# Attention and a mixer on one core: 128 stationary columns for the scores, a spread-out first pair, and block sums issued elsewhere

## The chip, the cores and the metric

The kernel runs on one core of one Trainium2 chip. The metric is the device time of one execution in microseconds (us). Each kernel was run several times; "fast" runs alone are compared, and all runs here were of that state or single.

Words used below: a *pair* is two heads of attention, and also the two score matmuls of them that run side by side; a *score group* is four score matmuls, that is two such pairs one after the other. A *row tile* is the part of the array's 128 rows that a matmul uses: 64 rows for a score matmul, 128 for most others. The *excess* between two matmuls is the distance of their starts less the steady distance of such matmuls. The *first-layer stretch* and the *output stretch* of a batch are its parts before and after the first matmul of the second layer. The *gain* is the multiplication of a transposed q by the norms' weights on DVE.

## The reference, cut to what matters

```python
def _attn_ref(q, k, v, g_q, g_k):            # q, k, v: 8 batches, 12 heads, 448 tokens, 64 per head
    q_n, k_n = rmsnorm(q, g_q), rmsnorm(k, g_k)
    scores = 1/sqrt(64) * q_n @ k_n.T
    attn = softmax(scores)
    return attn @ v

def _moe_ref(x, U, V, w_ch1, w_ch2):         # x: 8 x 448 x 768, the attention's output
    u = x + (x.T @ U @ V).T                  # mixing over tokens, rank 32
    return u + relu(u @ w_ch1) @ w_ch2       # 768 -> 3072 -> 768
```

## The kernel before

Everything runs in bf16 on the tensor engine (PE). While PE does the two layers of batch b, the attention of batch b+1 is woven in: a list of small items (scores of a pair of heads, exponentials on ScalarE (ACT), values, norms on VectorE (DVE)) with weights is spread over a share `FA` of the layers' work. A batch has six pairs of heads; p counts pairs over all batches.

```python
P, SP, D = 128, 112, 64
FA, FM, NPE, FA0 = (0.74, 0.77), 0.09, 14, 0.66

def scores(p, kcs):                          # two heads of 64 rows each, side by side in the array
    qT, kT = qkTs[p][:, 0], qkTs[p][:, 1]
    for kc in kcs:
        sc = ps_s.tile([SP, 2, 512], FP32, tag="s")
        for hh in range(2):
            pp = slice(hh * D, (hh + 1) * D)
            nc.tensor.matmul(sc[:, hh, 0:S], kT[pp, kc * SP:(kc + 1) * SP], qT[pp, :], start=True, stop=True)
        scs[p, kc] = sc

def gains(p):                                # DVE, after the transposing DMA of pair p has landed
    if p >= NPE:
        nc.vector.tensor_scalar(qkTs[p][:, 0], qkTs[p][:, 0], gg, None, OP.mult)

def attention(b, extra={}):                  # ... cut to the items that matter here
    for p in range(b * 6, b * 6 + 6):
        add(2 if p == 6 else 1, scores, p, (0, 1))
        add(0, expo, p, 0)
        add(.5, expo, p, 1)
        if p + 1 < NP and (p + 1 >= NPE or not odd):
            add(.5, transposes, p + 1)       # for p + 1 >= NPE a transposing DMA
        # ...
        if p % 6:
            add(2, values, p - 1, 0)         # matmuls into o, then DVE: reciprocal, x, xs
        # ...
        add(1, scores, p, (2, 3))
        add(0, expo, p, 2)
        add(.5, expo, p, 3)
        # ...
        if p + 1 < NP:
            add(0, gains, p + 1)
        # ...
        if p % 6:
            add(1.5, values, p - 1, 1)
```

The second layer of most rows is done by a scheme of seven block products in place of eight (`pair`), which needs sums of blocks of the activations hT on DVE:

```python
def act_sums(i, c0, c1):
    A11, A21, A22 = (hTe[:, c0:c1, k, t * P:(t + 1) * P] for k, t in ((0, i), (0, i + 1), (1, i + 1)))
    nc.vector.tensor_tensor(S1[:, c0:c1], A21, A22, OP.add)
    nc.vector.tensor_tensor(A21, A21, A11, OP.subtract)

def mlp(b):
    for hc in range(0 if b else 4, KH):      # first layer, 24 pieces of 128 columns
        # ... six matmuls into ph; even hc: relu on ACT, odd hc: relu on DVE
        if b and hc in (7, 15, 21, 23):
            act_sums(0, *{7: (0, 4), 15: (4, 8), 21: (8, 11), 23: (11, 12)}[hc])
        yield n
    # ... second layer: odd batches (N=512) two pairs, even ones (N=384) a single block row and a pair
    #     yield from pair(b, 0, lambda: act_sums(2, 0, NC))
```

## Time and profile before

| | before |
|---|---|
| median time, 6 runs beside the changed kernel | 587.84 us (586.63 to 591.5) |
| profiled execution, span | 584.4 us, granted clock 1.0 in all slices |
| busy: PE, DVE, ACT | 565.6, 395.0, 279.1 us |
| score groups on PE (outside the head) | 84 |

The page's first lines and its chain of waits, of the kernel before; the busy line gives us, share of the span and count:

```profile
PE 565.6 (97%) x4613; PEld 313.4 (54%) x4613; DVE 395.0 (68%) x811; ACT 279.1 (48%) x413; POOL 78.3 (13%) x122
...
PE 82%; DVE 11%; ACT 4%; issue 1%; DMA 1%; POOL 1%; DVEq 0%; POOLq 0%; ACTq 0%
```

PE is the bound. But "97% busy" is not "97% streaming", since a matmul's duration overlaps the next one's. The useful number is the distance from one matmul's start to the next. In steady state a 128x384 matmul follows another after 162 ns, although each is given 326 ns. Where the distance is larger, PE lost time. For the scores that happens three times per group. The timeline of the kernel before around one score group (start, us, engine, line, operation, idle of that engine before it):

```profile
332.43 0.67 PE L299 MATMUL o<-va,E 112*128 112x65 bf16 x16
333.03 0.18 PEld L273 LDWEIGHTS <-qkT 64*112 64x112 bf16 x4
333.03 0.58 PE L273 MATMUL sc<-qkT 64*112 64x448 bf16 x4
...
333.55 1.74 PEld L477 LDWEIGHTS <-w1b 128*128 128x128 bf16 x12 [0.34 <-issue]
333.55 2.12 PE L477 MATMUL ph<-u,w1b 128*128 128x384 bf16 x12
```

The weight load of the next matmul normally starts together with the matmul before it. Here the load after the group sat idle for 0.34 us for no reason that the profile shows ("issue"), and so did the first load of most groups. The groups of instructions of the kernel before (busy us, mean ns, then idle time of the engine before them):

```profile
L477 PEld LDWEIGHTS <-w1b 128*128 128x128 bf16 x1128 | 103.0, 98 | 106.6 <-issue 20.1
...
L273 PE MATMUL sc<-qkT 64*112 64x448 bf16 x384 | 60.0, 373 | 5.7 <-DVE rec L302 2.1
...
L273 PEld LDWEIGHTS <-qkT 64*112 64x112 bf16 x384 | 19.3, 124 | 37.3 <-issue 32.7
```

The score loads take 124 ns for 112 columns, the others 98 ns for 128: fewer columns, longer. And here are the waits of PE that have a named cause (total us, times, longest):

```profile
PE sc L273 <- DVE rec L302: 2.1, 3, 0.9
PE sc L273 <- DVE qkT L265: 1.7, 3, 0.6
PE o L299 <- DVE xs L306: 1.6, 3, 0.5
PE sc L273 <- ACT E L278: 1.2, 4, 0.4
```

The first two come once each in batches 2, 4 and 6 (second and first pair of the next batch's attention), the third once each in batches 1, 3 and 5 (value outputs behind the 0.94 + 1.55 us of block sums). One wait of DVE itself matters later, at the gain, for the transposing DMA:

```profile
DVE qkT L265 <- DMA qkT<-qkn: 2.3, 3, 0.9
```

### The profile page before, as it was taken

How to read it: one execution, taken by the hardware profiler on the slowest of the kernel's cores; microseconds unless marked ns; L12 is line 12 of the kernel's file. 1: busy time of each engine (PE TensorE's matmuls, PEld its weight loads, DVE VectorE, ACT ScalarE, POOL GpSimd, SP SyncE). 2: the span in 40 equal slices, each digit the busy share in tenths (PEclk: the TensorE clock that was granted, in tenths of full speed). 3: DMA queues.
4: the chain of work that ended last, by engine and by line, in shares of the span. 5: the costliest groups of instructions: out<-in, count | busy, mean ns of one | idle time of the engine just before them, and what ended most of it. 6: DMA issues, size and time to landing. Idle time of an engine off the chain costs nothing.

```text
span 584.4 us, 11372 instructions
## 1 busy us (share of the span) xinstructions
PE 565.6 (97%) x4613; PEld 313.4 (54%) x4613; DVE 395.0 (68%) x811; ACT 279.1 (48%) x413; POOL 78.3 (13%) x122
## 2 busy tenths in 40 slices
PE   7899999999999999999999999999999999999997
PEld 2465556544555556544555555644455555654464
DVE  5868987399775788656776588746677477453452
ACT  4957661276622774176631766256651475302200
POOL 4652411000020000000020001000011000000010
PEclk9999999999999999999999999999999999999999
DMA  9999999352554446525545355646425441040021
GB/s 218 244 239 235 223 152 203 82 112 47 106 156 103 110 102 134 139 61 115 118 119 101 75 125 127 148 98 127 109 54 147 94 96 33 28 109 0 1 55 54
DMA packets 103648, 67.22 MB, mean 115 GB/s; under 512 B 54716, under 2 KB 102060, under 8 KB 103596
## 3 DMA queue, kind: packets, MB, share of 16 engines
q1 hardware_dynamic: 93988, 56.77, 41.9%
q0 software_dynamic: 9376, 9.44, 9.9%
q8 instruction: 36, 0.59, 0.4%
q10 hardware_dynamic: 232, 0.30, 0.2%
q14 instruction: 16, 0.13, 0.1%
HBM read 52.19 MB, written 11.01 MB: 108 GB/s over the span
## 4 chain that ended last, share of the span: by engine, by line
PE 82%; DVE 11%; ACT 4%; issue 1%; DMA 1%; POOL 1%; DVEq 0%; POOLq 0%; ACTq 0%
PE ph L477 33%; PE pb L404 8%; PE po L404 8%; PE o L299 8%; PE pa L404 7%; PE sc L273 7%; PE pe L404 6%; ACT E L278 3%; DVE qkn L244 2%; PE pu L337 2%; DVE rstd L231 1%; PE warm L741 1%; DVE hT L400 1%; DVE S L399 1%; DVE x L303 1%
## 5 line engine op out<-in xcount | busy, mean ns | idle before, releaser
L477 PE MATMUL ph<-u,w1b 128*128 128x512 bf16 (+1 forms) x1128 | 232.5, 353 | 0.5 <-DVE qkT L259 0.3
L278 ACT ACTIVATE E<-sc 112x896 bf16<-112x896 f32 x184 | 159.3, 915 | 54.8 <-PE sc L273 54.2
L477 PEld LDWEIGHTS <-w1b 128*128 128x128 bf16 x1128 | 103.0, 98 | 106.6 <-issue 20.1
L404 PEld LDWEIGHTS <-hT 128*128 128x128 bf16 x1080 | 101.5, 98 | 71.2 <-issue 7.5
L480 ACT ACTIVATE hT<-ph 128x384 bf16<-128x384 f32 (+1 forms) x95 | 51.7, 546 | 148.0 <-PE ph L477 145.5
L482 DVE TENSOR_SCALAR hT<-ph 128x512 bf16<-128x512 f32 (+1 forms) x93 | 58.0, 624 | 58.5 <-PE ph L477 57.9
L299 PEld LDWEIGHTS <-E 112*128 112x128 bf16 x1472 | 58.4, 98 | 17.3 <-DVE xs L306 3.1
L273 PE MATMUL sc<-qkT 64*112 64x448 bf16 x384 | 60.0, 373 | 5.7 <-DVE rec L302 2.1
L299 PE MATMUL o<-va,E 112*128 112x65 bf16 x1440 | 61.0, 194 | 1.6 <-DVE xs L306 1.6
L244 DVE TENSOR_TENSOR qkn<-qk,rstd 112x512 bf16<-112x512 f32 x84 | 55.7, 701 | 7.2 <-ACT rstd L237 4.0
L702 POOL COPY scratch<-qkn 1x1 bf16<-1x1 bf16 x44 | 11.1, 251 | 312.0 <-DVE qkn L244 310.3
L404 PE MATMUL po<-w2b,hT 128*128 128x384 bf16 x288 | 52.0, 326 | 0.6 <-DVE hT L482 0.6
L231 DVE TENSOR_REDUCE rstd<-sq 112x16 f32<-112x1024 f32 x40 | 48.5, 1212 | 4.6 <-ACT sq L223 3.9
L404 PE MATMUL pa<-w2b,hT 128*128 128x384 bf16 x264 | 49.5, 326 | 0.0
L404 PE MATMUL pb<-Tw,hT 128*128 128x384 bf16 x264 | 48.0, 326 | 0.0
L273 PEld LDWEIGHTS <-qkT 64*112 64x112 bf16 x384 | 19.3, 124 | 37.3 <-issue 32.7
L223 ACT ACTIVATE sq<-qk 112x1024 f32<-112x1024 f32 x36 | 38.3, 1064 | 0.4 <-ACT hT L480 0.4
L303 DVE TENSOR_TENSOR x<-o,rec 128x192 bf16<-128x192 f32 x96 | 34.3, 357 | 3.7
L302 DVE RECIPROCAL rec<-o 128x4 f32<-128x4 f32 x96 | 17.1, 178 | 29.2 <-PE o L299 29.0
L439 POOL TENSOR_TENSOR o<-o,x 128x384 f32<-128x384 f32 x11 | 12.6, 1144 | 163.0 <-DVE o L438 163.0
L419 ACT ACTIVATE pb<-pa 128x384 f32<-128x384 f32 x11 | 5.2, 474 | 50.2 <-PE pa L404 50.2
L339 DVE TENSOR_TENSOR x<-pu,x 128x768 bf16<-128x768 f32 (+1 forms) x27 | 23.3, 865 | 7.2 <-PE pu L337 7.0
(106 smaller groups left out, 447.4 us busy)
## 6 DMA issues: line engine op xcount, KB each, us to landing
qk<-in_q_dram SPq DMA_DIRECT2D x21, 448.0 KB, 6.0
vt<-in_v_dram SPq DMA_DIRECT2D x20, 448.0 KB, 4.7
qk<-in_k_dram SPq DMA_DIRECT2D x19, 448.0 KB, 3.8
w2b<-in_moe_w_ch_dram POOLq DMA_DIRECT2D x6, 768.0 KB, 12.0
w1b<-in_moe_w_ch_dram POOLq DMA_DIRECT2D x2, 1536.0 KB, 22.0
out_dram<-o SPq DMA_DIRECT2D x15, 168.0 KB, 2.4
out_dram<-o SPq DMA_DIRECT2D x16, 144.0 KB, 2.1
out_dram<-o SPq DMA_DIRECT2D x15, 120.0 KB, 2.1
```

The costliest lines, as they stand in the source:

```text
L223: nc.scalar.activation(sqs[t, s][:, hs], qks[t, s][:, hs], AF.Square)
L231: nc.vector.tensor_reduce(rstds[t][:, s, hs].rearrange("p h j -> p (h j)"), sqs[t, s][:, hs].rearrange("p h (j d) -> p (h j) d", d=D), AX, ...
L244: nc.vector.tensor_tensor(qkn[:, s].rearrange("p j h d -> p h j d"), qks[t, s][:, hp].rearrange("p h (j d) -> p h j d", d=D), rstd[:, s, h ...
L273: nc.tensor.matmul(sc[:, hh, 0:S], kT[pp, kc * SP:(kc + 1) * SP], qT[pp, :], start=True, stop=True)
L278: nc.scalar.activation(E_of(p)[:, :, PAD + kc * S:PAD + (kc + 1) * S], scs.pop((p, kc))[:, :, 0:S], AF.Exp, scale=float(D) ** 0.5)
L299: nc.tensor.matmul(o[:, i, :], E[:, hh, c:c + P], va[:, hl, kc, :], start=(kc == 0), stop=(kc == NJ - 1))
L303: nc.vector.tensor_tensor(x3[:, :, d0:d0 + D], o[:, t0:t0 + 3, 0:D], rec[:, t0:t0 + 3].rearrange("p c -> p c ()").to_broadcast([P, 3, D]), ...
L339: nc.vector.tensor_add(xv, pu[rows, 0:n, 0:HALF], xv)
L404: nc.tensor.matmul(ps, lhs[:, c, :], rhs[:, c, :], start=first and c == 0, stop=last and c == NC - 1, skip_group_check=again)
L477: nc.tensor.matmul(ph, w1b[:, dc, hc * P:(hc + 1) * P], u[:, dc, :], start=(dc == 0), stop=(dc == KD - 1))
L480: nc.scalar.activation(hT[:, hc, 0:n], ph, AF.Relu)
L482: nc.vector.tensor_relu(hT[:, hc, 0:n], ph)
```

## The change

Three things, and no instruction more or less: the stationary operand of the scores gets 128 columns instead of 112, so that its load can be a fast one (the 16 extra columns are the next tokens', or q's at the end, and their rows of the result are not read; k and q change places so that there is something behind k). The first pair of a batch, which has no values to go with it, gets two idle items, so its exponentials and norms do not pile up. And the block sums move: in the first layer they go behind the next ACT relu, inside a pair the two sums are issued at two places.

```diff
@@ load @@
-                                  (q, k)[s][b, h0 + h:h0 + h + n].rearrange(...))
+                                  (k, q)[s][b, h0 + h:h0 + h + n].rearrange(...))
@@ transposes and gains: index 0 and 1 of qkT exchanged, cut @@
@@ scores @@
-        qT, kT = qkTs[p][:, 0], qkTs[p][:, 1]
+        qT, kT = qkTs[p][:, 1], qkTs[p].rearrange("d s n -> d (s n)")
-            sc = ps_s.tile([SP, 2, 512], FP32, tag="s")
+            sc = ps_s.tile([P, 2, 512], FP32, tag="s")
-                nc.tensor.matmul(sc[:, hh, 0:S], kT[pp, kc * SP:(kc + 1) * SP], qT[pp, :],
+                nc.tensor.matmul(sc[:, hh, 0:S], kT[pp, kc * SP:kc * SP + P], qT[pp, :],
@@ expo @@
-        ... scs.pop((p, kc))[:, :, 0:S], ...
+        ... scs.pop((p, kc))[0:SP, :, 0:S], ...
@@ act_sums, split into act_sum1 (S1) and act_sum3 (A21) @@
@@ pair @@
         store(b, i + 1, 1, o22)
-        if then:
-            then()
+        if more:
+            act_sum1(i + 2, 0, NC)
@@
         store(b, i, 1, o12)
+        if more:
+            act_sum3(i + 2, 0, NC)
@@ mlp @@
-            if b and hc in (7, 15, 21, 23):
-                act_sums(0, *{7: (0, 4), 15: (4, 8), 21: (8, 11), 23: (11, 12)}[hc])
+            if b and hc in (8, 16, 22, 23):
+                act_sums(0, *{8: (0, 4), 16: (4, 8), 22: (8, 11), 23: (11, 12)}[hc])
@@ attention @@
             if p % 6:
                 add(2, values, p - 1, 0)
+            elif b > 1:
+                add(1, idle)
@@
             if p % 6:
                 add(1.5, values, p - 1, 1)
+            elif b > 1:
+                add(1, idle)
```

More of the change, by code (lines that the diff above doesn't have):

```diff
@@ L198, in load @@
                 nc.sync.dma_start(qks[t, s][:, h:h + n],
-                                  (q, k)[s][b, h0 + h:h0 + h + n].rearrange("h (p j) d -> p h (j d)", j=NJ))
+                                  (k, q)[s][b, h0 + h:h0 + h + n].rearrange("h (p j) d -> p h (j d)", j=NJ))
     def load_v(t):
@@ L257, in transposes @@
                 nc.tensor.transpose(pt.rearrange("d s (j p) -> d (s j) p", j=NJ)[:, i, :], qkn[:, i, :], ident[:SP, :SP])
-            nc.vector.tensor_scalar(qkT[:, 0], pt[:, 0], gg, None, OP.mult)
-            nc.vector.tensor_copy(qkT[:, 1], pt[:, 1])
+            nc.vector.tensor_scalar(qkT[:, 1], pt[:, 1], gg, None, OP.mult)
+            nc.vector.tensor_copy(qkT[:, 0], pt[:, 0])
         else:
@@ L264, in gains @@
         if p >= NPE:
-            nc.vector.tensor_scalar(qkTs[p][:, 0], qkTs[p][:, 0], gg, None, OP.mult)
+            nc.vector.tensor_scalar(qkTs[p][:, 1], qkTs[p][:, 1], gg, None, OP.mult)
     def scores(p, kcs):
-        qT, kT = qkTs[p][:, 0], qkTs[p][:, 1]
+        qT, kT = qkTs[p][:, 1], qkTs[p].rearrange("d s n -> d (s n)")
         for kc in kcs:
-            sc = ps_s.tile([SP, 2, 512], FP32, tag="s")
+            sc = ps_s.tile([P, 2, 512], FP32, tag="s")
             for hh in range(2):
                 pp = slice(hh * D, (hh + 1) * D)
-                nc.tensor.matmul(sc[:, hh, 0:S], kT[pp, kc * SP:(kc + 1) * SP], qT[pp, :],
+                nc.tensor.matmul(sc[:, hh, 0:S], kT[pp, kc * SP:kc * SP + P], qT[pp, :],
                                  start=True, stop=True)
@@ L277, in expo @@
     def expo(p, kc):
-        nc.scalar.activation(E_of(p)[:, :, PAD + kc * S:PAD + (kc + 1) * S], scs.pop((p, kc))[:, :, 0:S],
+        nc.scalar.activation(E_of(p)[:, :, PAD + kc * S:PAD + (kc + 1) * S], scs.pop((p, kc))[0:SP, :, 0:S],
                              AF.Exp, scale=float(D) ** 0.5)
@@ L394, in weight_sums, with act_sum1, act_sum3 @@
         nc.vector.tensor_tensor(dst, x, y, OP.subtract)
+    def act_sum1(i, c0, c1):
+        A21, A22 = (hTe[:, c0:c1, k, (i + 1) * P:(i + 2) * P] for k in range(2))
+        nc.vector.tensor_tensor(S1[:, c0:c1], A21, A22, OP.add)
+    def act_sum3(i, c0, c1):
+        A11, A21 = (hTe[:, c0:c1, 0, t * P:(t + 1) * P] for t in (i, i + 1))
+        nc.vector.tensor_tensor(A21, A21, A11, OP.subtract)
     def act_sums(i, c0, c1):
-        A11, A21, A22 = (hTe[:, c0:c1, k, t * P:(t + 1) * P] for k, t in ((0, i), (0, i + 1), (1, i + 1)))
-        nc.vector.tensor_tensor(S1[:, c0:c1], A21, A22, OP.add)
-        nc.vector.tensor_tensor(A21, A21, A11, OP.subtract)
+        act_sum1(i, c0, c1)
+        act_sum3(i, c0, c1)
     def product(ps, lhs, rhs, first, last, again=False):
@@ L407, in product, with pair @@
                 yield HALF
-    def pair(b, i, then=None):
+    def pair(b, i, more=False):
         x = x_tiles(b)
@@ L498, in mlp @@
         elif par:
-            yield from pair(b, 0, lambda: act_sums(2, 0, NC))
+            yield from pair(b, 0, True)
             yield from pair(b, 2)
@@ L510, in add, with idle @@
             items.append((weight, lambda: fn(*args)))
+        def idle():
+            pass
         def sums(p, n):
```

## The prediction

> **What bounds the kernel now.** The tensor engine. The page's busy table gives PE 565.6 of 584.4 us (97%), DVE 68%, ACT 48%; granted clock 1.0 in every slice; the chain of waits that ended last is 82% PE. Adding up start-to-start distances of the matmuls, back-to-back streaming explains about 537 us; about 39 us is excess. A third is in the first 45 us (warm-up, waits for ACT). In the body there are two kinds.
>
> 1. Switching between the score matmuls (64 rows x 112 columns) and everything else; the order has 107 such groups. In the timeline around 333 us: the last 128x384 matmul starts 255 ns before the first score pair (its own stream is 162, so +93); the first score pair takes 393 ns instead of the 349 of the second (+44); the next matmul begins 285 ns after the second pair (187 is its stream, so +98). About 235 ns per group.
> 2. Real waits, about 6.5 us: three of 0.5 us of the value matmuls behind DVE block sums (near 305 us), three of 0.6 us in a batch's first pair (near 328, behind DVE's gain), three of 0.6 to 0.9 us in the second pair (near 338, behind DVE's relu, sums and gain), and four short ones for ACT's exponential.
>
> **What the change does.** (a) Stationary operand of scores 112 -> 128 columns. The Trainium skill, "TensorE: Matmul & The Clock Gate", section "Weight-path perf modes", says the fast weight load is on when the number of weights is 128 and the type is not FP32. The trace agrees: 128-column loads are read as four chunks of 32 and take 98 ns, the 112-column ones are read as one run and take 123 to 126. The 16 more columns cost no streaming time. (b) Idle weight in the first pair of batches 2 to 7. (c) Block sums move after the next ScalarE relu, and the 0.94 + 1.55 us sums in a pair are split around the block's next output. No instruction's work is added; the order of instructions shows DVE's relu going ahead of sums and gains.
>
> **How much counts.** Of kind 1 only the +44 is the weight load itself; I expect about 12 (what the first matmul after a score group shows: 336 against 326). 32 ns x about 85 groups outside the ACT-bound head = 2.8 us. I expect the +93 and +98 to stay: they look like draining the array when the row tile changes. Evidence: one transposing group with 32 rows and 128 columns, loaded fast, is followed by a 128-row load 99 ns after its last matmul, where 25 is the rhythm, although that load waits for no semaphore; a fast load alone did not remove it. If this is wrong and fast loading removes the drains, another 16 to 20 us go.
> Of kind 2, I expect 5 of 6.5 us gone; a quicker PE and denser later pairs give some back.
>
> **Predicted: 580 us** (before 587.8), 8 in 10 between 572 and 584. Faster by over 2%: 0.22; within 2%: 0.77; slower: 0.01.
>
> **What would show it.** Score weight loads near 98 ns; first score pair about 360 instead of 393, so mean of the score matmuls 373 -> about 355; the issue-idle of 32.7 us before score weight loads and 20.1 before the first-layer loads roughly unchanged (they fall to a few us if I am wrong about draining). Waits of PE for DVE (reciprocal, x, gain) falling from about 5.5 us to under 2. Busy times of DVE and ACT unchanged.
>
> **What would make it wrong.** Drains that belong to slow weight loads, not to row tiles (under 565 us); two fast loads for the two row halves not running together (gain (a) gone); the idle items squeezing later pairs so that DVE or ACT holds PE there (585 or more).

## The result, and the profile after

| | before | after |
|---|---|---|
| median of 6 runs | 587.84 us | 581.32 us (579.54 to 581.84) |
| ratio, 95% interval | | 0.9874 [0.9843, 0.9906] |
| span of the profiled execution | 584.4 us | 579.7 us |
| head (first matmul to first first-layer matmul of batch 0) | 42.26 us | 43.80 us |
| body (from there to the last matmul) | 534.16 us | 527.92 us |

A ratio is the mean time of one kernel's fast runs over that of the other's of the same rounds, so it is not quite the ratio of the medians. The result is correct, 1.3% faster, which counts as the same at the 2% mark. Head and body are worked out from the starts of the matmuls in the trace.

The same lines after. Page and chain of the changed kernel:

```profile
PE 562.7 (97%) x4613; PEld 306.5 (53%) x4613; DVE 397.8 (69%) x811; ACT 280.2 (48%) x413; POOL 78.3 (14%) x122
...
PE 85%; DVE 7%; DMA 3%; ACT 2%; issue 1%; POOL 1%; DVEq 0%; POOLq 0%; ACTq 0%
```

Its timeline around the corresponding score group:

```profile
333.31 0.11 PEld L273 LDWEIGHTS <-qkT 64*128 64x128 bf16 x4 [0.32 <-issue]
333.31 0.55 PE L273 MATMUL sc<-qkT 64*128 64x448 bf16 x4
...
333.79 0.76 PEld L488 LDWEIGHTS <-w1b 128*128 128x128 bf16 x6 [0.37 <-issue]
```

Its groups, and the waits of PE:

```profile
L488 PEld LDWEIGHTS <-w1b 128*128 128x128 bf16 x1128 | 102.8, 98 | 108.6 <-issue 22.5
...
L273 PE MATMUL sc<-qkT 64*128 64x448 bf16 x384 | 56.1, 358 | 3.3 <-ACT E L278 1.1
...
L273 PEld LDWEIGHTS <-qkT 64*128 64x128 bf16 x384 | 12.5, 94 | 35.6 <-issue 30.7
```

```profile
PE sc L273 <- ACT E L278: 1.1, 3, 0.5
PE sc L273 <- DVE qkT L265: 0.8, 3, 0.3
PE o L299 <- DVE xs L306: 0.7, 2, 0.5
...
PE sc L273 <- DVE rec L302: 0.5, 1, 0.5
```

Three readings. The score load fell from 124 to 94 ns and the whole score group from 0.58 to 0.55 us, but the idle "issue" of the loads around score groups stayed: 32.7 to 30.7 and 20.1 to 22.5 us. The three named waits on DVE fell from 5.4 to 2.0 us together. And one on DVE itself has grown: before, it waited at a gain for the transposing DMA for 2.3 us in all; now (waits of DVE, changed kernel) for

```profile
DVE qkT L265 <- DMA qkT<-qkn: 6.0, 5, 1.9
```

and DMA has gone from 1% to 3% of the chain.

**A finer measure.** Since the first 45 us vary most from run to run, I cut the trace at the first first-layer matmul of each batch. Batch 7, where nothing of the change acts, lasts 58.21 to 58.23 us in all the experiments, batches 3 and 5, which run the same program, agree within 0.03 us in every kernel, and batch 0 takes 63.9 to 65.8 us with no clear relation to the edits (why is not shown). So the sum of batches 1 to 7 is the fairest measure of one profile. Batches 2 and 4 also run the same program, and still differ by up to 1.1 us within one profile (63.52 and 62.39 us in e2). So the odd sums below are firm, while a difference of a microsecond in the even sum, or in the whole, can be chance unless batches 2 and 4 show it alike.

| kernel | batches 1, 3, 5 | batches 2, 4, 6 | sum 1 to 7 | against before |
|---|---|---|---|---|
| before | 225.07 | 186.11 | 469.39 | |
| changed | 220.96 | 184.40 | 463.57 | -5.8 |
| e1, columns alone | 224.16 | 185.58 | 467.96 | -1.4 |
| e2, idle items alone | 224.21 | 186.57 | 469.00 | -0.4 |
| e3, first-layer sums alone | 225.02 | 185.06 | 468.30 | -1.1 |
| e4, split sums alone | 222.92 | 186.68 | 467.81 | -1.6 |
| e8, changed without idle items | 221.81 | 183.97 | 464.00 | -5.4 |
| e9, changed, DMA earlier | 220.96 | 182.46 | 461.63 | -7.8 |
| e10, changed, idle items selected | 220.93 | 183.05 | 462.19 | -7.2 |
| e11, e9 and e10 together | 220.96 | 184.09 | 463.26 | -6.1 |
| e12, changed, wider spread | 220.97 | 184.27 | 463.47 | -5.9 |
| e7, changed, gain later | 232.17 | 191.35 | 481.74 | +12.4 |

### The profile page after: what moved, and what is told of

Same layout as the page of the kernel before. It is cut to its first block, busy times and chain, and to the rows that moved or that the text cites. A ratio compares the mean times of both kernels' runs of the same rounds, so it can differ in the third digit from the quotient of the medians.

```text
span 579.7 us, 11362 instructions
## 1 busy us (share of the span) xinstructions
PE 562.7 (97%) x4613; PEld 306.5 (53%) x4613; DVE 397.8 (69%) x811; ACT 280.2 (48%) x413; POOL 78.3 (14%) x122
## 4 chain that ended last, share of the span: by engine, by line
PE 85%; DVE 7%; DMA 3%; ACT 2%; issue 1%; POOL 1%; DVEq 0%; POOLq 0%; ACTq 0%
PE ph L488 35%; PE pb L413 10%; PE po L413 8%; PE o L299 7%; PE pe L413 7%; PE sc L273 7%; PE pa L413 6%; DMA qkT<-qkn 2%; DVE qkn L244 2%; ACT E L278 2%; PE pu L337 2%; PE warm L759 1%; DVE rstd L231 1%; PE first L732 1%; PE pt L257 1%
## 5 line engine op out<-in xcount | busy, mean ns | idle before, releaser
L488 PEld LDWEIGHTS <-w1b 128*128 128x128 bf16 x1128 | 102.8, 98 | 108.6 <-issue 22.5
L273 PE MATMUL sc<-qkT 64*128 64x448 bf16 x384 | 56.1, 358 | 3.3 <-ACT E L278 1.1
L273 PEld LDWEIGHTS <-qkT 64*128 64x128 bf16 x384 | 12.5, 94 | 35.6 <-issue 30.7
## 6 DMA issues: line engine op xcount, KB each, us to landing
w1b<-in_moe_w_ch_dram POOLq DMA_DIRECT2D x2, 1536.0 KB, 22.5
```

The costliest lines, as they stand in the source:

```text
L273: nc.tensor.matmul(sc[:, hh, 0:S], kT[pp, kc * SP:kc * SP + P], qT[pp, :], start=True, stop=True)
L488: nc.tensor.matmul(ph, w1b[:, dc, hc * P:(hc + 1) * P], u[:, dc, :], start=(dc == 0), stop=(dc == KD - 1))
```

## The experiments

My theory: the columns pay only by the load itself, some 30 ns a group; the larger gaps before and after a score group are the array draining because the row tile changes from 128 to 64 rows and back; the rest of the gain comes from DVE being less in the way, and part of it is given back in the denser later pairs. The rivals: the columns are the whole gain; or the gaps belong to slow loads, or to the scores' operands and buffers.

### e1_cols: the columns alone

```diff
-                                  (q, k)[s][b, h0 + h:h0 + h + n].rearrange(...))
+                                  (k, q)[s][b, h0 + h:h0 + h + n].rearrange(...))
-            sc = ps_s.tile([SP, 2, 512], FP32, tag="s")
+            sc = ps_s.tile([P, 2, 512], FP32, tag="s")
-                nc.tensor.matmul(sc[:, hh, 0:S], kT[pp, kc * SP:(kc + 1) * SP], qT[pp, :],
+                nc.tensor.matmul(sc[:, hh, 0:S], kT[pp, kc * SP:kc * SP + P], qT[pp, :],
 (and the exchanged indices in transposes, gains and expo, as in the change)
```

> Only part (a): 128 stationary columns of k for the scores. Theory A (only the load itself counts): score weight loads near 95 ns, first score pair of a group 360 instead of 393 ns, and the excess before and after a score group stays at 93 to 96 ns; 2.5 to 3.5 us faster than before (ratio 0.994 to 0.996). Rival B (columns are the whole gain of the change, the rest is cosmetic): 6 to 7.5 us faster (0.987 to 0.990).

Measured: ratio 0.9906 [0.987, 0.9942], median 585.06 us, but against runs of the kernel before that ranged from 586.72 to 592.93 (see the head, below), so the interval reaches into the ranges of both theories. The trace decides. The body is 532.31 us, 1.85 less; batches 1 to 7 are 1.4 less. The excess before a group is 96 ns (94 before), after it 93 (93 before); the median distance from the first to the second pair fell from 233 to 200 ns. The waits are those of before (2.2, 1.9 and 1.7 us in the three lines shown). The groups of weight loads of e1:

```profile
L477 PEld LDWEIGHTS <-w1b 128*128 128x128 bf16 x1128 | 103.0, 98 | 108.5 <-issue 22.1 <-DVE qkT L259 0.2
L273 PEld LDWEIGHTS <-qkT 64*128 64x128 bf16 x384 | 12.9, 94 | 38.2 <-issue 31.0 <-DMA qkT<-qkn 3.0 <-DVE qkT L259 2.1
```

So the columns are about a quarter to a third of the gain, and the gaps stayed (31.0 and 22.1 us of "issue" against 32.7 and 20.1). Rival B fell. The same longer runs of the kernel before stand behind the ratios of e2, e3 and e4: all three ratios lie below the range expected for them, e2's on the rival's side (0.996 or below), but each interval reaches into the expected range, and the trace, not the ratio, decides there too.

### e2_idle: the idle items alone

```diff
+            elif b > 1:
+                add(1, idle)     # in place of each of the two value items of a first pair
```

> Only part (b): idle items in the first pair of batches 2 to 7. Theory A: the waits of PE near 328 (0.6 us, three times) and ACT's at 253 and 390 shrink, 2 us gained, but later pairs are denser and a new wait of about 0.7 to 1 us appears in the output stretch of each even batch (as in the changed kernel near 366), so only 0 to 1.5 us net (ratio 0.997 to 1.000). Rival: the full 2.5 us or more is kept (0.996 or below).

Measured: 0.9953 [0.9911, 0.9995], median 587.52 us; batches 1 to 7 only 0.4 us less. The wait for the gain (L265) fell from 1.7 to 0.2 us, and others grew in its place (waits of PE, e2):

```profile
PE o L299 <- DVE xs L306: 2.3, 5, 0.5
PE sc L273 <- DVE rec L302: 2.3, 2, 1.9
```

DVE's own wait at the gains for the transposing DMA went from 2.3 to 11.4 us (waits of DVE, e2):

```profile
DVE qkT L265 <- DMA qkT<-qkn: 11.4, 10, 2.8
```

Batches 1, 3 and 5 gained 0.9 us together. Batches 2, 4 and 6 went from 61.85, 61.86 and 62.40 us to 63.52, 62.39 and 60.66: two are worse, one is better. So about half of what the odd batches gained is given back in the even ones, and the net lies in theory A's 0 to 1.5 us; within the scatter of the even batches it may also be nothing.

### e3_mlpsums: the first-layer sums alone

```diff
-            if b and hc in (7, 15, 21, 23):
-                act_sums(0, *{7: (0, 4), 15: (4, 8), 21: (8, 11), 23: (11, 12)}[hc])
+            if b and hc in (8, 16, 22, 23):
+                act_sums(0, *{8: (0, 4), 16: (4, 8), 22: (8, 11), 23: (11, 12)}[hc])
```

> Only the block sums of the first layer moved behind the next ScalarE relu. Theory A: the waits near 338 (0.6 to 0.9 us, three times) become about half, because the relu now goes ahead and sums and gain still stand before the next scores: 0.5 to 1.5 us gained (0.9975 to 0.999). Rival: nothing, as the first pair's delay sets that wait.

Measured: 0.9946 [0.9904, 0.9988], median 586.56 us; batches 1 to 7 are 1.1 us less, nearly all of it in the even ones (1.05). The wait "sc <- DVE rec", 2.1 us in the kernel before, is gone from the list of this kernel; the other two stayed at 1.7 and 1.6 us. Batches 2 and 4 show it alike (0.57 and 0.58 us less), batch 6 does not (0.1 more, although its wait of 0.9 us is gone too). The cause is the one expected, and the wait went wholly rather than by half.

### e4_split: the sums inside a pair alone

```diff
-        if then:
-            then()                       # both sums, 0.94 + 1.55 us, behind o22
+        if more:
+            act_sum1(i + 2, 0, NC)       # behind o22
 ...
+        if more:
+            act_sum3(i + 2, 0, NC)       # behind o12, one product later
```

> Only the two block sums inside a pair issued at two places. Theory A: the waits of the value matmuls near 305 (0.54 us on PE, 0.6 to 0.7 in start-to-start distance, three times) vanish: 1.5 to 2 us gained (0.9965 to 0.9975). Rival: the time is given back at the next place where DVE is behind, gain under 0.7 us.

Measured: 0.9928 [0.9888, 0.9969], median 586.06 us; batches 1, 3, 5 are 2.15 us less, 0.7 us each, and batch 6 alone was 0.55 longer. The wait "o <- DVE xs" is gone from the list and the other two are unchanged (2.1, 1.7). As expected.

The four parts make 4.5 us one by one and 5.8 together. e8, below, shows that the three parts without the idle items do 5.4 together and 4.1 singly. That two causes stand behind each other in DVE's order, so that taking away one leaves part of the wait to the other, would explain it, but is not shown: differences of 1.3 us between sums of single profiles are near the scatter of the even batches.

### e5_rows128 and e6_rows112: what the gaps around a score group are

```diff
-                pp = slice(hh * D, (hh + 1) * D)
+                pp = slice(0, P)          # all 128 rows; e5 on e1 (128 columns), e6 on the kernel before (112)
```

> Wrong result on purpose: as e1 (128 stationary columns, fast load), but each score matmul reads all 128 rows, both heads at once, so there is no row tile of 64. Theory (the gaps of about 94 ns before and after a score group are the array draining when the row tile changes): both gaps fall to under 10 ns of excess; the two matmuls of a pair no longer run side by side (189 ns apart instead of 3), so the kernel is about 384/2 x 0.19 = 36 us of PE longer, less about 20 us of gaps: some 598 to 606 us. Rival (the gaps belong to something else about the scores, such as waiting for their PSUM buffers or operands): 90 ns stay on both sides.

> Wrong result on purpose: as before (112 stationary columns, slow load), with all 128 rows. Theory (row tile alone makes the gap): no gap of 94 ns here either, at most a few tens of ns for the slow load itself. Rival (a change between fast and slow loads makes it too): 94 ns stay before and after each score group, as in the kernel before.

Their outputs are wrong, which doesn't matter for the times. One execution each, at a granted clock of 1.0: 594.81 and 596.21 us, against a median of 587.31 for the kernel before. The groups of weight loads of e5:

```profile
L477 PEld LDWEIGHTS <-w1b 128*128 128x128 bf16 x1128 | 107.8, 98 | 98.2 <-issue 0.9
L273 PEld LDWEIGHTS <-qkT 128*128 128x128 bf16 x384 | 35.0, 97 | 36.5 <-issue 7.4 <-DVE qkT L259 1.8
```

and of e6, with the slow load:

```profile
L477 PEld LDWEIGHTS <-w1b 128*128 128x128 bf16 x1128 | 107.9, 98 | 96.4 <-issue 1.1
L273 PEld LDWEIGHTS <-qkT 128*112 128x112 bf16 x384 | 46.9, 130 | 28.4 <-issue 6.9 <-DVE qkT L259 1.8
```

The idle "issue" before the first-layer loads fell from 20.1 to 0.9 and 1.1 us, before the score loads from 32.7 to 7.4 and 6.9. Worked out from the starts, the median excess is 0 ns before and 0 ns after a score group in both. (The idle time of a load counts the streaming of the matmul before it as well, so it is larger than the loss.) Thus the gaps come with the 64-row matmuls, whichever way the weights are loaded; a slow load between full-row matmuls makes none in the median. One thing e5 and e6 change along with the row tile: the two heads no longer run side by side. That this is not the cause is suggested by the 32-row transposes of the kernel before, which start 25 ns apart, not side by side, and whose successor still starts 103 ns after the last of them. This agrees with the Trainium skill, "TensorEngine Tiling (Array Packing)", section "Tiling Modes", key properties: changing the tiling mode drains the tensor engine. The page gives no cost; here it is 93 to 96 ns each way, 84 times two, about 16 us of the body.

The total was mis-expected: not 598 to 606 but 594.8 us for e5. From e1 to e5 a score group grew by 147 ns (mean 658 to 805 with its waits, sum over 84 groups 12.3 us), where I had counted about 180; and some of PE's waits elsewhere shrank when PE became slower (batches 1 to 7 grew by 8.8 us, where their 72 groups alone make 10.6). The drains cannot be saved in this way: two full-row matmuls of 189 ns in place of a concurrent pair cost more than the drain.

### e7_gainlate: the gain behind the value outputs

```diff
-            if p + 1 < NP:
-                add(0, gains, p + 1)
             ...
             if p % 6:
                 add(1.5, values, p - 1, 1)
             sums(p, 3)
+            if p + 1 < NP:
+                add(0, gains, p + 1)
```

> The changed kernel, with the gain of the next pair issued on DVE after the second value group of the previous pair instead of ahead of it. Theory: the time that the spread-out first pair gives back in the output stretch of even batches (28.4 to 28.7 us against 27.1 before) comes from DVE standing at that gain, waiting 1.8 us for the transposing DMA, with the value outputs behind it; so the stretch returns to about 27.1 to 27.4 us and the kernel gains 3 to 4 us on the changed one (ratio to before about 0.981). Rival: the first score group of the next pair then waits for its gain instead, and nothing or less than 1 us is gained.

Measured: 600.62 us, ratio 1.0213 [1.018, 1.0245]. The rival holds, with more force than expected. The longest of PE's waits in e7:

```profile
PE sc L273 <- DVE qkT L265: 17.4, 21, 2.3
```

Behind the value outputs, the gain of the next pair cannot start before PE has done the values and DVE their reciprocal, outputs and block sums; PE then reaches the next scores and waits for it. Some of the 12.4 us, 1.7 by my estimate, is the clock: after gaps of 2.3 and 1.9 us on PE in batch 1 the trace shows a granted clock of 0.5 for 3.4 us, from 143.6 us on. The place in DVE's order that looked wasteful (waiting 1.8 us for a DMA) was on the whole the right one.

### e8_noidle: the changed kernel without the idle items

```diff
-            elif b > 1:
-                add(1, idle)     # both places
```

> The changed kernel without the idle items. From the parts (body from the first first-layer matmul to the end: before 534.2, columns alone -1.9, first-layer sums alone -1.3, split sums alone -1.8): body about 529.0, against 527.9 of the changed kernel, so 0.5 to 1.5 us slower than it. Rival (the idle items only pay together with the others, or only cost): more than 2 us slower, or faster than it.

Measured: 582.61 us, 0.9915 [0.9884, 0.9947]. The body is 527.91 us against 527.92 of the changed kernel; batches 1 to 7 are 464.00 against 463.57. In these two profiles the idle items are worth 0.4 us on top of the others: batches 1, 3, 5 gain 0.3 each and batch 6 gains 1.0, but batch 2 loses 1.3 (61.04 to 62.33) and batch 4 0.1. The odd batches are firm; the even ones differ by about their scatter. Neither expectation is exact: the 0.5 to 1.5 us that I expected to lose is 0.0 in the body.

### e9_early and e10_idlesel: two ways to keep what is given back

```diff
 e9:  the transposing DMA ahead of the current scores
+            if NPE <= p + 1 < NP:
+                add(0, transposes, p + 1)
             add(2 if p == 6 else 1, scores, p, (0, 1))
 ...
-                add(.5, transposes, p + 1)
+                add(.5, *((transposes, p + 1) if p + 1 < NPE else (idle,)))
 e10: idle items in batches 2, 4, 6 and 7 only
-            elif b > 1:
+            elif b > 1 and (b % 2 == 0 or b == B - 1):
                 add(1, idle)
```

> The changed kernel with the transposing DMA of the next pair issued ahead of the current pair's first scores instead of after them (pairs from 13 on; an idle item keeps its weight). Theory (the give-back in even output stretches is DVE held 1.8 us at the gain by that DMA): the DMA starts 1 to 1.5 us sooner, DVE's wait for it falls under 0.5 us, the even output stretches go from 28.4 to 28.7 us towards 27.1 to 27.4, body about 525 against 527.9. Rival (the give-back is only the same work done in a later and denser stretch, DVE being full there): the DVE wait falls but the stretch stays within 0.3 us of 28.4.

> The changed kernel with the idle items only in batches 2, 4, 6 and 7, that is, not where they were worth less in the first-layer stretch (0.4 to 0.9 us) than they gave back after it (1.0 to 1.7). From the stage times of the changed kernel with and without them: even stretches of batches 2 and 4 as without idle items (33.96 and 27.1 to 27.4), odd ones and batch 6 as with them (40.01, 33.51, 32.71, 27.9): body about 526.5, 1.4 us less than the changed kernel. Rival: the stretches are coupled (what is left over from one batch shows in the next) and nothing is gained.

Measured: e9 579.1 us, 0.985 [0.9818, 0.9882], body 526.74; e10 578.47 us, 0.9843 [0.981, 0.9876], body 526.53. By their medians both are below the changed kernel (581.32 us) too, but that one ran in other rounds and its interval, [0.9843, 0.9906], overlaps theirs, so the whole times do not settle it. DVE's wait at the gain in e9:

```profile
DVE qkT L265 <- DMA qkT<-qkn: 2.6, 3, 1.0
```

I had expected under 0.5 us, against 6.0 in the changed kernel. The trace says where it helped. The two longest of these waits in the changed kernel, 1.86 us at 231 us and 1.83 us at 366 us, stand at the last pair of batches 2 and 4, where the DMA was issued 4.4 and 4.2 us after the pair's first scores; in e9 it is issued 2.1 us after them, and both waits are gone, with PE's waits of 0.5 and 0.2 us for DVE's output ("o <- DVE xs") just behind. At the other pairs of these batches, though the item stands earlier in the program, the DMA is issued no sooner. So the DMA was part of what held DVE, and the even batches fell from 184.40 to 182.46 us. The output stretches alone (27.66, 27.95 and 27.83 us, from 28.73, 28.39 and 27.90) recovered less than half of what I had expected. I had read those stretches wrongly, too: a wider spread moves attention work from the first-layer stretch into the output stretch, so a longer output stretch is not all loss. Only a whole batch can be compared, as in the table. e10 did what its sum said (526.5 expected and measured), batches 2 and 4 alike.

### e11_both and e12_wide: do they add up, and is it density?

```diff
 e11: both edits of e9 and e10
 e12: FA = (0.775, 0.77) in place of (0.74, 0.77), in the changed kernel
```

> The two improvements on the changed kernel together: idle items only in batches 2, 4, 6 and 7, and the transposing DMA of the next pair ahead of the current scores. Each alone left a body of 526.7 (early DMA) and 526.5 us (selected idle items). If they remedy the same give-back, the body is 526.0 to 526.6, the even batches as with the selection and batch 6 as with the early DMA; if they add up, 525.3 or less.

> The changed kernel with the attention of the next batch spread over 0.775 instead of 0.74 of an even batch's work, so that the later pairs are no denser than before the idle items came in (44 weights in place of 42, 4.8% more). Theory (the give-back is the density of the later pairs): the even output stretches return from 28.4 to 28.7 us to 27.1 to 27.5 and the first-layer ones keep 33.1 to 33.6, body about 524.5 against 527.9. Rival (it comes from where the gain stands relative to its DMA, whatever the density): the stretches stay within 0.4 us of 28.4 or the wait only moves.

Measured: e11 580.28 us, 0.986 [0.9825, 0.9895], body 527.88; e12 580.87 us, 0.9886 [0.9844, 0.9928], body 528.58. Both miss their expectations. In e11 nothing adds up: batches 2 and 4 take 61.39 and 62.19 us (61.04 and 61.11 in e10), the wait of PE's scores for the gain is 2.8 us, against 1.0 in e9 and 1.5 in e10, and DVE's wait for the DMA is again that of the changed kernel:

```profile
DVE qkT L265 <- DMA qkT<-qkn: 6.0, 6, 2.3
```

Its two longest waits, 1.6 and 2.3 us, stand at the third pair of batches 2 and 4. There the DMA is issued as long after the scores as in e10 (0.57 us), but it lands 6.5 and 7.2 us after its issue, against 6.1 in e10. So it is the landing time that differs; whether the edits cause that, or it is chance from one execution to the next, one profile each cannot say. In e12 the even batches sum to 184.27, as in the changed kernel (184.40); the output stretches are even longer (29.57, 28.84, 29.44), the first-layer ones shorter, and PE now waits for the transposed input of the next batch's first layer (waits of PE, e12):

```profile
PE ph L488 <- DMA u<-x: 2.0, 3, 1.1
```

This new wait, as large as the effect looked for, spoils the test: less density may have helped and the later mixing have taken it back. So e12 gained nothing, but whether density is the cause of the give-back is not settled. What exactly makes batch 2 of the changed kernel 1.3 us longer than that of e8 stays open in part; its output stretch is 1.7 us longer, and holds the wait of 1.86 us for the DMA that e9 took away.

### Why the times of one kernel differ by 2 to 6 us

The profile of e3 has a head of 48.79 us, and the body is quiet. Its stretches, 20 to 40 us (busy us and count of PE, PEld, DVE, ACT, POOL; granted clock; DMA share; GB/s):

```profile
20.00:24.00 4.00, 3.67 (x26) 1.87 (x27) 3.53 (x7) 2.32 (x4) 1.80 (x5) 0.67 1.14 209
24.00:28.00 4.00, 4.00 (x39) 2.11 (x38) 3.08 (x8) 3.01 (x4) 2.98 (x5) 0.50 1.19 223
28.00:33.00 5.00, 4.89 (x47) 2.85 (x45) 3.21 (x10) 3.82 (x7) 1.22 (x4) 0.50 1.18 238
33.00:40.00 7.00, 7.00 (x84) 4.68 (x82) 3.93 (x15) 4.21 (x6) 5.78 (x5) 0.61 1.16 244
```

Half the clock for some 17 us, from 21.4 to 38.5 us; the profile of the kernel before has 1.00 in all of them. What came before it, in the timeline of e3 (DVE's norms of the second half, and POOL's squares):

```profile
11.09 2.99 DVE L244 TENSOR_TENSOR qkn<-qk,rstd 112x512 bf16<-112x512 f32 x2
...
11.22 2.30 POOL L225 TENSOR_TENSOR w2b<-qk 112x1024 f32<-112x1024 f32 x1 [6.67 <-DMA qk<-in_q_dram]
```

and the same in the kernel before:

```profile
11.59 1.34 DVE L244 TENSOR_TENSOR qkn<-qk,rstd 112x512 bf16<-112x512 f32 x2
...
9.89 1.89 POOL L225 TENSOR_TENSOR w2b<-qk 112x1024 f32<-112x1024 f32 x1 [5.34 <-DMA qk<-in_q_dram]
```

A load landed later, POOL's product began while DVE was in its own, DVE took 2.99 instead of 1.34 us, and PE waited 1.42 us for it. The Trainium skill, "SBUF — State Buffer", section "SBUF: two separate sides", says that DVE and GpSimd share one pair of ports by an exclusive lock, which a DVE operation with two inputs in SBUF contends for when the GpSimd operation reads SBUF; both are such operations here, and the durations fit. This chain is read from two traces and was not tested by a run. Its size is clear: executions of the kernel before, of e2, e3 and e4 with a mean clock of 0.984 to 0.993 took 587 to 593 us, where those at 0.999 or 1.0 mostly took 584 to 588 (one of the kernel before took 590.56 at 1.0, so the clock is not all of it). The intervals above are wide in part for that reason.

## Why the prediction was right, point by point

- **580 us, 8 in 10 between 572 and 584.** Measured 581.32. Right.
- **The drains stay.** Right, and shown: with fast loads the idle "issue" stayed at 30.7 and 22.5 us, and e5 and e6, with full rows, removed most of it (7.4 and 0.9, 6.9 and 1.1 us). The one transposing group of 32 rows in the trace before was a good witness. Its strength was that its next load waited for no semaphore and still came late.
- **(a) 2.8 us by 32 ns in 85 groups.** The mechanism was right and the term too large: 1.85 us in the body of e1, 1.4 in batches 1 to 7. The distance inside a group was 230 to 234 ns in 73 of the 84 groups of the kernel before and fell by 33 ns; in four it was 204 ns already, and in seven a real wait stood there (400 ns and more). The gap before a group grew by 2 ns. Over all groups that makes 2.2 us (a mean of 26 ns by 84), of which part was lost again in waits elsewhere.
- **First score pair 393 to 360 ns, score loads to 98, mean of the score matmuls to 355.** Measured 360, 94 and 358. Right. The loss that I named as a risk, two fast loads not running together, did not come: the two matmuls of a pair still start 3 to 4 ns apart.
- **(b) and (c), 5 of 6.5 us.** The body lost 6.24 us, of which 1.85 are the columns; 4.4 remain. Nearly right. The three waits for DVE fell to 2.0 us in sum (I had said under 2). The share was not where I saw it: the idle items, to which I gave the first-pair waits, are worth 0.4 us net in batches 1 to 7, and the two moves of sums nearly all the rest. That the joint term fits although the shares in it were wrong is luck. The total is not: both terms were too large, by about 1.0 and 0.6 us, and no error hid another.
- **A quicker PE and denser later pairs give some back.** They did in batch 2; density is not shown to be the reason (e12 could not settle it), and the DMA that DVE waits for at the gain has a part (e9). I had not foreseen that DVE's wait for the transposing DMA would grow from 2.3 to 6.0 us.

## What to carry to other kernels

A switch between a 64-row and a 128-row tile costs the tensor engine about 95 ns each way here, however the weights are loaded: count the switches, and think of grouping what shares a tile (not tried here). A fast load of 128 columns saved only the exposed part of the load, 33 ns once per group. Spreading one stage moved its waits to others here (e2): compare whole periods, not the stage that became shorter, and where the start of a kernel is noisy, compare stretches of the trace, and look first at how far two that run the same program differ.

## What the Trainium skill lacked or had wrong

- "TensorEngine Tiling (Array Packing)", Tiling Modes: it says that a change of mode drains the engine, but not what that costs. Here 94 to 96 ns before and 92 to 93 ns after each group of 64-row matmuls (medians), and 94 and 96 ns around the 128x32 ones of the mixing.
- "TensorE: Matmul & The Clock Gate", LDWEIGHTS: its formula (columns over 1.2) gives an estimate of 93 ns for a load of 112 columns, where the trace has 123 to 126 ns. And what a stream loses by a load, which the page does not give, was less: the exposed part was 44 ns for the slow load (393 against 349 ns) and 11 for the fast one (360 against 349), and 0 where the load is hidden.
- The same page, "Why this matters for your kernels": it warns of idle gaps of over about 3 us. In the head of these kernels the clock fell to half with no gap that long before it: the longest were 1.08 us (the changed kernel's profile) and 1.42 us (e3), with other short gaps around them. The length of one gap does not decide it: at the same place as in the changed kernel, gaps of 0.95 us (the kernel before) and of 1.07 us (e9, e11, e12) left the clock at 1.0.
- No page says that a fast load makes no difference to the drain: with 128 columns it was 96 and 93 ns, with 112 it was 94 and 93.
